# Decay attention with a gated MLP on one Trainium2 core: one decay row of 512 a head, masked in place, and four decay and transposed tiles

## The chip, the cores and the metric

The program runs on one core of one Trainium2 chip, in one launch. The metric is the device time in microseconds (us). The kernel before took 532.27 us, the median of three runs (524.27, 532.27 and 534.39 us).

The engines are named as the profile names them: PE (matrix multiply), PEld (its weight loads), DVE (vector), ACT (scalar and activation), POOL (general purpose), SP (here it only issues DMAs). Each engine runs its own instructions in the order in which they stand in the program, and waits where an operand is not ready.

## The reference

```python
def _attn_ref(q, k, v, f):                       # q, k, v: (8, 8, 576, 64); f: (8, 8, 576)
    scores = 1/sqrt(64) * q @ k^T
    log_f = np.log(np.clip(f, 0.0001, 1.0))
    cum = np.cumsum(log_f, axis=-1)
    decay = cum[:, :, :, None] - cum[:, :, None, :]
    scores = np.where(causal, -1e9, scores + decay)      # causal: key after query
    scores = scores - np.max(scores, axis=-1, keepdims=True)
    attn = np.exp(scores)
    attn = attn / (np.sum(attn, axis=-1, keepdims=True) + 1e-09)
    return attn @ v

def _moe_ref(x, w_val, conv_w, w_out):           # x: (8, 576, 512), heads side by side
    gate_pre = sum over 5 taps of conv_w[k] * x shifted by k
    gate = 1.0 / (1.0 + np.exp(-gate_pre))
    return (gate * (x @ w_val)) @ w_out
```

All arrays are float32. The term `cum[query]` of a row of scores is the same for all keys, so the softmax takes it away again: any number that is constant along a row may be added to the row's decays.

## The kernel before, in words

Two heads of a batch entry make a pair; there are 32 pairs, four to a batch entry. A pair's 576 queries are four blocks of 128, j = 0 to 3, with 128(j + 1) keys each, and a rest of 64 queries with all 576 keys; the rests of both heads share one 128-row tile. The stages of a pair are these.

- Load: `Xr` (queries and keys), `vt` (values), and for pairs 2 to 31 the decays, by a DMA that copies one row of the DRAM table `decd` to 128 partitions: `dm`, 1280 columns a head (the four blocks' 128, 256, 384 and 512 keys behind each other, each block with its own reference), and `dl`, 576 columns for the rest. There are three `dm` tiles.
- Mask: POOL writes -8e9 over the upper triangle of the four diagonal blocks of a `dm` tile, in two `affine_select` instructions of 128x256 (L314), once the tile has landed. The rest's 64 columns get `tri` added (L317, DVE or POOL).
- S: PE multiplies queries by keys into PSUM (`banks`). From pair 4 on the operands are split in a high and a low part (`Xh`, `Xl`; L268 and L397) and three products are made.
- Reduce (L479, DVE): adds the decays to the scores in place and returns each row's extreme; a small instruction then reads that out (`negm`). Exp (L483, ACT) makes `P` and the row sums.
- PT: PE transposes `P` (L511, L529, L530); ACT or DVE copies the result to `pt` (L268), of which there are three.
- PV: PE multiplies `vt` by `pt`; DVE multiplies the result by the inverse row sums (L580), which come as a DMA broadcast through DRAM (`rzd`), into `x`. `xh` and `xl` are its split.
- Convolution: five taps on `x` into `gate` (L616 on DVE for four of them), then a tanh on ACT.
- MoE of a batch entry once its four pairs are through: Mv (`xh`, `xl` by `w_val`), gating on DVE (L648), a split into `hh` and `hl`, Mo (by `w_out`), output copies (L689, L691) and DMAs.

At the start DVE clips `f`, ACT takes the logarithm (L348), ACT loads its second table of functions (L349), DVE makes the running sum (L350), and `ref` (L352) and five scaled copies (L359 on ACT, L361 on DVE) make the table `st`, which two DMAs write to `decd`. Pairs 0 and 1 don't wait for `decd`: PE adds their decays to the scores by a selecting matrix `pick`, and their reduction reads a `dm` tile that holds zeros and the mask. The two weight matrices are decoded on DVE and ACT in eight chunks (L705 to L717) into high and low parts.

What order the instructions stand in on each engine, and which engine does an instruction that several could do, is given by the string `TABLE`: five characters or so for each step, made beforehand by a planner. Every step that `plan_...` adds has a list of what it reads and writes; the table only may order them.

Of the kernel before, what the change touches and what calls it, by code (L numbers as in the profile page):

```python
# [7 lines left out]
F32 = mybir.dt.float32  # L8
# [19 lines left out]
NXR = 3  # L28
R0 = 16
# [5 lines left out]
SW = 1280  # L35
XZ, XK, XW = 512, 640, 1216
# [11 lines left out]
423M15A41s21u14z21t24F24D23R003S11v35I37z44A14G14B24E14H0177t43A21y13x001z24M24C13y23D31A24-
023T034Y054143B13U13P063_44I21H45y449004U034Z11B24O23C31C14J14N13Q24K27v41D24L14P13E25_051E24T24t41G34a21S447016027K17L3482540475g24V15h25525845H31F15
647I13F26117B45e14d15f14W004X17J34b14c35S0135X21K24_11J15V25J046755T250025U15Z25118O45K25L18I48Q45O25P15Q252005R15a44e25M21M25c41L25313G25N11N11O27x45  # L50
Y15k077F382045W17H3832a345-16223H28X16b018Z38411P21Q11R37V0027G38-25l263036c16416f0646r18K46g15E46q26j46h4a147-
26p15i056s19X48W365071U18Y2670321468169015j25m21V29h047_15o16618026a17W27Y27X11X29i2bi47Z16l44f25n36d061W26e19j16n41Y18e008U3980734g2ba49d24h27M014651
Z28116v027R28f1aa1ab39e1ac1ad37S17T27U17N28M47O17P26t008c05992a938d17Q19Z47D48a0686018b28V39a16w21-
22038528716u26I05a7388068915p26x18i0278s18u1bg48v25q26y28j18m48_001649021_18g028t2942bo38k43I16J09119f26F076G09g19_46K2bp2bq3a839629518q4aw058h19719b2
9c19p029q18o46H26L1br1ax2ay1di48w049225r28y00231do45s29318x2an0724i1bc45t1ae06513as28z2ao29l009m1at16N04aq2af29k26z16O0aj28S4al2am1ah26M3ag16Q006R09n0
# [121 lines left out]
def tile_decay_attention_gated_mlp(  # L177
# [643 lines left out]
```

## Time and profile before

| | |
|---|---|
| runs | 524.27, 532.27, 534.39 us |
| profiled execution, its own time | 527.19 us |
| its span, first to last instruction | 525.3 us |
| granted TensorE clock, mean | 0.999 |
| PE, PEld busy | 504.5, 443.6 us |
| DVE, ACT, POOL busy | 438.7, 347.6, 224.3 us |
| DMA traffic | 103.39 MB |

A busy time is the time in which at least one instruction of the engine was under way. Matmuls overlap each other and their ends are modelled. An engine's idle time before an instruction is put down to what ended it.

### The profile page before, as it was taken

Reading aid. Unit: us, or ns where it says so; the run is one execution under the profiler, and the core shown is the slowest. Engines: PE = TensorE matmul, PEld = TensorE weight load, DVE = VectorE, ACT = ScalarE, POOL = GpSimd, SP = SyncE. Lnnn points to the kernel's source line nnn. Section 1 sums busy time; section 2 is a strip of 40 time slices with the busy share of each in tenths; the row PEclk is TensorE's granted clock in tenths of the full one; section 3 lists DMA queues with packets and bytes.
Section 4 is the critical chain, followed back from the end, with each engine's and each line's share of the span. In section 5 each row is a group of like instructions: output and inputs, shape, how many; then the busy total and the mean of one; then the engine's idle time right before and its main releaser. Section 6 shows DMA issues by size and latency. Waiting matters only on the chain. (4 is left out here: it accounts for less than half of the span.)

```text
span 525.3 us, 12611 instructions
## 1 busy us (share of the span) xinstructions
PE 504.5 (96%) x4392; PEld 443.6 (84%) x4392; DVE 438.7 (84%) x1186; ACT 347.6 (66%) x991; POOL 224.3 (43%) x293
## 2 busy tenths in 40 slices
PE   7887999999989999999999998999999999999997
PEld 6555789989988898987899887999898997998885
DVE  6899999898889888898797897898888897868680
ACT  6799998885667665767757776778657664543111
POOL 5248565646352261563326752565454531140110
PEclk9999999999999999999999999999999999999999
DMA  6979898565664676576757386766677544320022
GB/s 212 307 237 325 282 282 288 187 225 157 224 214 136 233 238 190 154 247 198 213 202 271 126 262 219 235 178 225 205 243 259 204 157 144 121 69 2 22 81 100
DMA packets 35022, 103.39 MB, mean 197 GB/s; under 512 B 5072, under 2 KB 5328, under 8 KB 34960
## 3 DMA queue, kind: packets, MB, share of 16 engines
q1 hardware_dynamic: 34960, 102.60, 60.0%
q8 instruction: 34, 0.56, 0.4%
q14 instruction: 28, 0.23, 0.2%
HBM read 92.52 MB, written 10.06 MB: 195 GB/s over the span
## 5 line engine op out<-in xcount | busy, mean ns | idle before, releaser
L483 ACT ACTIVATE P<-banks,negm 128x128 f32<-128x128 f32 (+3 forms) x256 | 133.8, 532 | 38.4 <-DVE negm L479 35.5
L479 DVE CUSTOM_DVE_ANT_0 banks<-banks,dm 128x384 f32<-128x384 f32 (+3 forms) x256 | 120.5, 512 | 10.1 <-PE banks L253 6.6
L268 ACT COPY pt<-banks 128x256 f32<-128x256 f32 (+2 forms) x235 | 94.5, 437 | 41.7 <-PE banks L511 22.7
L253 PE MATMUL banks<-xh,wall 128*128 128x288 f32 x512 | 113.2, 300 | 0.0
L616 DVE SCALAR_TENSOR_TENSOR gate<-x,cw,gate 128x576 f32<-128x576 f32 x128 | 108.9, 857 | 1.1
L253 PE MATMUL banks<-pt,vt 128*64 128x128 f32 (+2 forms) x1408 | 95.8, 290 | 1.9 <-ACT P L483 1.9
L253 PEld LDWEIGHTS banks<-pt,vt 128*64 128x64 f32 x1408 | 84.0, 137 | 13.8 <-ACT P L483 3.1
L511 PE MATMUL banks<-ident,P 128*128 128x128 f32 x640 | 89.0, 277 | 5.5 <-ACT pt L268 2.5
L253 PE MATMUL banks<-wall,hh 128*128 128x512 f32 x288 | 91.9, 400 | 2.0 <-ACT P L483 0.9
L314 POOL TENSOR_SCALAR_AFFINE_SELECT dm<-dm 128x256 f32<-128x256 f32 x122 | 57.6, 498 | 84.0 <-DMA dm<-decd 66.9
L253 PEld LDWEIGHTS banks<-xh,wall 128*128 128x128 f32 x512 | 85.0, 188 | 1.3 <-DVE h L648 0.3
L511 PEld LDWEIGHTS banks<-ident,P 128*128 128x128 f32 x640 | 71.1, 140 | 15.3 <-ACT P L483 4.0
L253 PE MATMUL banks<-xl,wall 128*128 128x288 f32 x256 | 75.4, 295 | 0.0
L397 POOL TENSOR_TENSOR Xl<-Xr,Xh 128x576 fp32r<-128x576 f32 (+1 forms) x41 | 63.0, 1545 | 19.9 <-ACT Xh L268 16.0
L253 PE MATMUL banks<-Xh 128*128 128x288 f32 (+4 forms) x280 | 59.2, 339 | 3.7 <-ACT Pl L483 1.7
L253 PEld LDWEIGHTS banks<-wall,hh 128*128 128x128 f32 x288 | 51.2, 188 | 11.7 <-DVE x L580 1.4
L253 PE MATMUL banks<-wall,hl 128*128 128x512 f32 x144 | 56.4, 391 | 0.0
L253 PE MATMUL banks<-Xh,Xl 128*128 128x288 f32 (+4 forms) x280 | 54.8, 315 | 0.1
L253 PE MATMUL banks<-Xl,Xh 128*128 128x288 f32 (+4 forms) x280 | 54.0, 313 | 0.0
L483 ACT ACTIVATION_READ_ACCUMULATOR P<-banks,negm 128x1 f32 x256 | 52.6, 205 | 0.0
L253 PEld LDWEIGHTS banks<-xl,wall 128*128 128x128 f32 x256 | 48.2, 188 | 0.5
L587 POOL TENSOR_TENSOR xl<-x,xh 128x576 fp32r<-128x576 f32 x20 | 29.2, 1462 | 44.7 <-ACT xh L268 41.0
(95 smaller groups left out, 726.0 us busy)
## 6 DMA issues: line engine op xcount, KB each, us to landing
dm<-decd SPq DMA_DIRECT2D x60, 640.0 KB
Xr<-in_x_dram SPq DMA_DIRECT2D x32, 608.0 KB
vt<-in_v_dram SPq DMA_DIRECT2D x32, 320.0 KB
x<-rzd SPq DMA_DIRECT2D x64, 144.0 KB
out_dram<-ot SPq DMA_DIRECT2D x36, 256.0 KB
dl<-decd SPq DMA_DIRECT2D x60, 144.0 KB
ot<-in_w_val_dram SPq DMA_DIRECT2D x2, 512.0 KB
wu<-in_w_val_dram SPq DMA_DIRECT2D x2, 512.0 KB
```

Of the source, the lines that this page charges most:

```text
L253: nc.tensor.matmul(out, lhsT=lhsT, rhs=rhs, start=start, stop=stop)
L268: (eng.copy if eng is nc.scalar else eng.tensor_copy)(out=out, in_=in_)
L314: nc.gpsimd.affine_select(out=t, in_=t, pattern=[[0, 2], [-1, P]], base=0, channel_multiplier=1, compare_op=ALU.is_ge, fill=-BIG)
L397: eng.tensor_tensor(out=Xl[r][:, a:e], in0=Xr[r][:, a:e], in1=Xh[r][:, a:e].bitcast(F32), op=ALU.subtract)
L479: nc.vector.tensor_tensor_reduce(out=sl, in0=sl, in1=add[:, o:o + ext], op0=ALU.add, op1=ALU.min, scale=-0.125, scalar=3.0e38, accum_out=n ...
L483: nc.scalar.activation(out=dst[:, o:o + ext], in_=bank(key)[:, c0:c0 + ext], func=AF.Exp, bias=negm[r][:, col], scale=-1.0, accum_out=zs[r ...
L511: nc.tensor.transpose(out=bank(key)[:, c:c + P], in_=Pt[m][:, BOFF[b] + P * j:BOFF[b] + P * j + P], identity=ident)
L587: any_("xl", {"POOL": 1.4, "DVE": 0.67}, p, lambda eng: eng.tensor_tensor(out=xl[s], in0=xv, in1=xh[s][:, :].bitcast(F32), op=ALU.subtract ...
L616: eng.scalar_tensor_tensor(out=gt, in0=src, scalar=wt_, in1=gt, op0=ALU.mult, op1=ALU.add)
```

## The change

Each head has one decay row of 576 columns with one reference (the running sum at key 288) in place of five pieces with five references. A pair's head loads only the first 512 columns (128x512, 256 KB, before 640 KB) into one of four `dm` tiles. All four blocks read that tile from its first column. The mask of block j is written over its last 128 columns right before its reduction, by POOL or by DVE (adding `tri4`): block 3 first, then 2, 1 and 0, since block 2 needs the columns that were masked for it, and block 3 needs the same columns unmasked. So each head has the chain mask, reduce, mask, reduce and so on, four of each. The groups of PSUM banks change to fit: blocks 3 and 2, then blocks 1 and 0.

At the start one DVE instruction makes the whole table, and one DMA writes it. The reduction of pairs 0 and 1 reads `mask` and `maskl`. There are four `pt` tiles. The `rzd` DMAs may be issued by ACT as well as by SP. POOL may do convolution taps of the first pairs (the new table gives it none). The whole order is new.

```diff
+REF = S // 2
+NDM = 4
+NPT4 = 4
...
 TABLE = """
-0240040430s010w000c20u040e20f10740g10v030b30F40t010Q40520h20H10i20932g001240k12i00K20n20l10m10z32r0570C33342e30j10o43540I20J20E32h00q40630L10B32n22o12
...
+0d20710930040430q030m010240e20o020520B40D10p010G20M40f10a30E20F20h20630H10I20u30z32Z40J22a002350i22c00j40K20L20O10P20b20R20g10S10X45v40Q20c32h22i12j22
...
-    decd = dram.tile([R, SW + S], F32, name="decd")
-    dm = tiles(NH, [P, SW], F32, "dm")
+    decd = dram.tile([R, S], F32, name="decd")
+    dm = tiles(NDM, [P, L0], F32, "dm")
...
-    pt = tiles(NH, [P, 1600], F32, "pt")
+    pt = tiles(NPT4, [P, 1600], F32, "pt")
...
-            load("dec", 2.3 if i < 6 else 2.05, p + 0.05 * h, dm[m], decd[2 * i + h:2 * i + h + 1, 0:SW].to_broadcast([P, SW]), dk, [("dm", m)])
+            load("dec", 0.85, p + 0.05 * h, dm[(2 * i + h) % NDM], decd[2 * i + h:2 * i + h + 1, 0:L0].to_broadcast([P, L0]), [("decd",)], [("dm", (2 * i + h) % NDM)])
...
-            def sel(m=m):
-                for lo, n, c in ((0, 256, 0), (256, 512, 384)):
-                    t = dm[m][:, lo:lo + 2 * n].rearrange("p (b c) -> p b c", b=2)[:, :, c:c + P]
-                    nc.gpsimd.affine_select(out=t, in_=t, pattern=[[0, 2], [-1, P]], base=0, channel_multiplier=1,
-                                            compare_op=ALU.is_ge, fill=-BIG)
-            pool("sel", 0.8, p + 0.2 + 0.05 * h, sel, [("dm", m)], [("dm", m)])
...
-    dve("st0", 0.12, z, lambda: nc.vector.tensor_scalar(out=ref, in0=cum[:, 0:L0 + 1:P], scalar1=8.0, scalar2=0.0, op0=ALU.mult, op1=ALU.add),
-        kc, [("ref",)])
...
-    for c in cuts:
-        cut(*c)
...
-        load("tabD", (0.35, 0.9)[n], z - 0.5, decd[r0:r1], st[r0:r1], [*ktab, *kst], [("decd", n)])
+    dve("cut0", 0.45, z, lambda: nc.vector.tensor_scalar(out=st, in0=cum, scalar1=cum[:, REF:REF + 1], scalar2=-8.0,
+        op0=ALU.subtract, op1=ALU.mult), kc, kst)
+    load("tabD", 0.5, z - 0.5, decd, st[0:R], kst, [("decd",)])
...
-    SG = (((0, 3, 0), (1, 3, 0), (0, 1, 0), (1, 1, 0)), ((0, 2, 0), (1, 2, 0), (0, 0, 384), (1, 0, 384)), ((None, 0, 224),))
+    SG = (((0, 3, 0), (1, 3, 0), (0, 2, 0), (1, 2, 0)), ((0, 1, 0), (1, 1, 0), (0, 0, 256), (1, 0, 256)), ((None, 0, 224),))
...
+                if u < 2 and not deep:
+                    def sel(eng, t=dm[md][:, ext - P:ext]):
+                        if eng is nc.gpsimd:
+                            eng.affine_select(out=t, in_=t, pattern=[[-1, P]], base=0, channel_multiplier=1, compare_op=ALU.is_ge, fill=-BIG)
+                        else:
+                            eng.tensor_tensor(out=t, in0=t, in1=tri4, op=ALU.add)
+                    any_("sel", {"POOL": 0.3, "DVE": 0.21}, pp - (0.3 if j == 3 else 0.0), sel, [*dkey, ("tri4",)], dkey)
...
-        load("rzw", 0.1, p + 0.03, rzd[i, :, L0:], rt[r][D + 2 * NB:], [("rt", r)], [("rzd", i, 1)])
+        load("rzw", 0.1, p + 0.03, rzd[i, :, L0:], rt[r][D + 2 * NB:], [("rt", r)], [("rzd", i, 1)], early=True)
```

The number and shape of PE's instructions stay as they were (3,630 matmuls as the program issues them). Of the other instructions, counted in the order as built: 60 broadcasts of 128x1280 become 60 of 128x512; 122 masks of 128x256 on POOL become 173 of 128x128 on POOL and 67 of 128x128 on DVE; DVE's output copies (L691) go from 16 to 7 and ACT's from 20 to 29; DVE's 128x512 copies of `pt` with four runs go from 16 to 7 and ACT's from 48 to 57; 25 of the 128 `rzd` DMAs are issued by ACT.

The start, on ACT (`h32` holds the convolution weights and `ot` the first chunk of `w_val`, both still coded; `Pl1` holds `f`). Before:

```order
L348 ACTIVATE Pl1_83<-Pl1_83 128x576
L349 ACT_TABLE_LOAD
L705 ACTIVATE gate1_112<-h32_113 128x20
L359 ACTIVATE gate0_111<-x321_94,ref_127 128x256
L359 ACTIVATE gate0_111<-x321_94,ref_127 128x384
L359 ACTIVATE gate0_111<-x321_94,ref_127 128x128
L359 ACTIVATE gate0_111<-x321_94,ref_127 128x512
L713 ACTIVATE h32_113<-h32_113,ebias_125 128x20
L483 ACTIVATE P0_79,zs0_91<-banks_126,negm0_89 128x256
```

and now:

```order
L714 ACTIVATE gate1_115<-h32_116 128x20
L350 ACTIVATE Pl1_85<-Pl1_85 128x576
L722 ACTIVATE h32_116<-h32_116,ebias_128 128x20
L714 ACTIVATE gate1_115<-ot_125 128x512
L351 ACT_TABLE_LOAD
L722 ACTIVATE ot_125<-ot_125,ebias_128 128x512
L478 ACTIVATE P0_81,zs0_94<-banks_129,negm0_92 128x384
```

Four table copies (L359) are gone; two instructions that need the first chunk of `w_val` (the fourth and sixth row) now stand ahead of the first exp.

The masks of pair 4, on DVE (`dm0` and `dm1` are its two heads now, `dm2` and `dm0` before). Before, the reductions stood in any order, with the masks long done:

```order
L479 ISA banks_126,negm0_89<-banks_126,dm2_70 128x256
L479 ISA negm0_89 128x1
L479 ISA banks_126,negm0_89<-banks_126,dm0_68 128x256
L479 ISA negm0_89 128x1
L479 ISA banks_126,negm0_89<-banks_126,dm2_70 128x512
L479 ISA negm0_89 128x1
L479 ISA banks_126,negm0_89<-banks_126,dm0_68 128x512
```

and now:

```order
L474 ISA banks_129,negm0_92<-banks_129,dm0_69 128x512
L474 ISA negm0_92 128x1
L474 ISA banks_129,negm0_92<-banks_129,dm1_70 128x512
L474 ISA negm0_92 128x1
L485 TENSOR_TENSOR dm0_69<-dm0_69,tri4_66 128x128
L474 ISA banks_129,negm0_92<-banks_129,dm0_69 128x384
L474 ISA negm0_92 128x1
L474 ISA banks_129,negm0_92<-banks_129,dm1_70 128x384
L474 ISA negm0_92 128x1
L625 SCALAR_TENSOR_TENSOR gate0_114<-x321_97,cw_67,gate0_114 128x576
L474 ISA banks_129,negm0_92<-banks_129,dm0_69 128x256
```

The two heads alternate, block 3 first. The mask of block 2 of the first head is one of the 67 on DVE; that of the second head, and the two of block 1, are POOL's. They stand there among POOL's other work (`wall` is a chunk of weights, `xl` and `Xl` are splits):

```order
L590 TENSOR_TENSOR xl1_109<-x321_97,xh1_103 128x576
L751 TENSOR_TENSOR wall_126<-gate1_115,wu_127 128x512
L483 AFFINE_SELECT dm1_70<-dm1_70 128x128
L483 AFFINE_SELECT dm0_69<-dm0_69 128x128
L483 AFFINE_SELECT dm1_70<-dm1_70 128x128
L483 AFFINE_SELECT dm3_72<-dm3_72 128x128
L483 AFFINE_SELECT dm0_69<-dm0_69 128x128
L483 AFFINE_SELECT dm1_70<-dm1_70 128x128
L392 TENSOR_TENSOR Xl0_79<-Xr0_75,Xh0_77 128x576
```

Each of these masks but the fourth row's now has to wait for the reduction of the block before it on DVE, and the next reduction waits for it.

The products of pair 3 (L580, then L583; `x320`), the last that batch entry 0 needs, on DVE. Before:

```order
L479 ISA banks_126,negm1_90<-banks_126,dm1_69 128x384
L479 ISA negm1_90 128x1
L268 COPY pt2_86<-banks_126 128x256
L580 TENSOR_TENSOR x320_93<-banks_126,x320_93 128x192
L717 TENSOR_SCALAR ot_122<-gate1_112 128x512
L490 TENSOR_SCALAR Pl0_82<-zs0_91 128x9
L491 RECIPROCAL Pl0_82<-Pl0_82 128x9
L580 TENSOR_TENSOR x320_93<-banks_126,x320_93 128x384
```

and now:

```order
L474 ISA banks_129,negm0_92<-banks_129,dm1_70 128x128
L474 ISA negm0_92 128x1
L583 TENSOR_TENSOR x320_96<-banks_129,x320_96 128x192
L583 TENSOR_TENSOR x320_96<-banks_129,x320_96 128x384
L492 TENSOR_SCALAR Pl0_84<-zs0_94 128x9
L493 RECIPROCAL Pl0_84<-Pl0_84 128x9
```

Counted from the start, DVE has 182 instructions ahead of the first of these two products before, and 174 now. Of each of the four decoding instructions L707, L709, L711 and L715 one fewer stands ahead of it now, of the reductions one of 128 and one of 384 columns fewer, and `ref` is gone.

## Rows read from the trace of the kernel before

**Rows 1.** The page: span, and each engine's busy time with its share.

```profile
span 525.3 us, 12611 instructions
PE 504.5 (96%) x4392; PEld 443.6 (84%) x4392; DVE 438.7 (84%) x1186; ACT 347.6 (66%) x991; POOL 224.3 (43%) x293
```

**Rows 2.** Stretches: length, busy us of PE, PEld, DVE, ACT, POOL; clock, DMA, GB/s.

```profile
0.00:10.00 10.00, 7.37 (x40) 5.98 (x42) 5.37 (x14) 5.76 (x10) 7.33 (x27) 1.00 0.61 207
10.00:60.00 50.00, 42.97 (x358) 31.16 (x355) 45.60 (x142) 45.63 (x132) 23.85 (x30) 1.00 0.90 286
40.00:80.00 40.00, 35.85 (x359) 29.77 (x357) 37.91 (x112) 39.62 (x112) 26.75 (x31) 1.00 0.92 295
100.00:450.00 350.00, 344.62 (x3096) 307.62 (x3094) 303.95 (x820) 237.06 (x698) 159.99 (x199) 1.00 0.63 206
450.00:500.00 50.00, 49.12 (x409) 44.94 (x408) 36.04 (x79) 17.87 (x42) 7.71 (x6) 1.00 0.16 56
```

**Rows 3.** The timeline of ACT at the start: start us, us, instruction.

```profile
5.82 1.28 ACT L349 ACT_TABLE_LOAD   x1
...
7.08 1.56 PE L253 MATMUL banks<-Xr 64*128 64x512 f32 x8 [1.21 <-DMA Xr<-in_x_dram]
...
9.74 0.47 ACT L483 ACTIVATE P<-banks,negm 128x256 f32<-128x256 f32 x1
...
10.80 0.68 ACT L705 ACTIVATE gate<-ot 128x512 f32<-128x512 uint32 x1
...
13.40 0.75 ACT L713 ACTIVATE ot<-ot,ebias 128x512 int32<-128x512 int32 x1
```

**Rows 4.** DVE by line and shape: xcount, busy us, mean ns, idle before.

```profile
L479 DVE CUSTOM_DVE_ANT_0 banks<-banks,dm 128x384 f32<-128x384 f32 x64 | 36.2, 576 | 3.9 <-PE banks L253 2.4 <-issue 0.4 <-POOL dm L314 0.3
...
L268 DVE COPY pt<-banks 128x512 f32<-128x512 f32 x29 | 19.6, 680 | 1.7 <-PE banks L511 1.4
L479 DVE CUSTOM_DVE_ANT_0 banks<-banks,dm 128x128 f32<-128x128 f32 x64 | 19.4, 312 | 0.8 <-ACT P L483 0.3 <-PE banks L253 0.2
...
L691 DVE TENSOR_SCALAR ot<-banks 128x512 f32<-128x512 f32 x16 | 10.9, 686 | 10.2 <-PE banks L253 5.4 <-DMA out_dram<-ot 4.6
...
L709 DVE SCALAR_TENSOR_TENSOR gate<-gate 128x512 f32<-128x512 int32 x8 | 5.6, 700 | 0.0
L662 DVE TENSOR_TENSOR hl<-h,hh 128x512 fp32r<-128x512 f32 x8 | 5.5, 684 | 0.0
...
L715 DVE SCALAR_TENSOR_TENSOR gate<-ot 128x512 int32<-128x512 int32 x4 | 3.0, 738 | 0.1
...
L317 DVE TENSOR_TENSOR dl<-dl,tri 128x64 f32<-128x64 f32 x10 | 2.5, 253 | 0.0
...
L711 DVE TENSOR_SCALAR ot<-ot 128x512 int32<-128x512 int32 x4 | 1.8, 446 | 0.4 <-ACT gate L705 0.4
L707 DVE TENSOR_SCALAR gate<-ot 128x512 int32<-128x512 int32 x4 | 1.7, 427 | 2.0 <-DMA ot<-in_w_val_dram 1.5 <-DMA ot<-in_w_out_dram 0.4
...
L352 DVE TENSOR_SCALAR ref<-x 128x5 f32<-128x5 f32 x1 | 0.4, 393 | 0.0
```

**Rows 5.** The instructions that write or read `dm`: who waited for them.

```profile
  POOL dm L314: 66.9, 23
...
  DVE banks L479: 1.1, 3
```

**Rows 6.** POOL by line and shape, as rows 4.

```profile
L314 POOL TENSOR_SCALAR_AFFINE_SELECT dm<-dm 128x256 f32<-128x256 f32 x122 | 57.6, 498 | 84.0 <-DMA dm<-decd 66.9 <-DVE x L580 6.8 <-DVE dl L317 5.9
L397 POOL TENSOR_TENSOR Xl<-Xr,Xh 128x576 fp32r<-128x576 f32 x22 | 32.8, 1493 | 14.5 <-ACT Xh L268 10.8 <-DVE Xh L268 3.4
...
L323 POOL TENSOR_SCALAR_AFFINE_SELECT ident<-ident 128x128 f32<-128x128 f32 x1 | 0.3, 292 | 0.1
```

**Rows 7.** Two DVE lines: duration ns least/median/most, first and last start.

```profile
L616 DVE SCALAR_TENSOR_TENSOR gate<-x,cw,gate x128: 756/814/1984, 42.0 to 501.0; 128x576 f32<-128x576 f32 x128
...
L490 DVE TENSOR_SCALAR Pl<-zs x32: 157/170/1512, 22.9 to 477.4; 128x9 f32<-128x9 f32 x32
```

More of the change, by code (lines that the diff above doesn't have):

```diff
@@ L28 @@
 NXR = 3
+NPT = 4
 R0 = 16
@@ L48 @@
[L48 to L55, printed above, removed]
@@ L324, in mk_ident @@
                                 compare_op=ALU.is_equal, fill=0.0)
-    cuts = [(i, BOFF[i], 0, EXT[i]) for i in (3, 1, 2, 0)] + [(NB, SW, 0, S)]
-    ref = const.tile([P, NB + 1], F32, name="ref")
     for h in range(2):
@@ L340, in tile_decay_attention_gated_mlp @@
     for i in range(ND):
[L341 to L344 removed]
+        pool("start", 1.25, z + 0.25, lambda i=i: mk_pick(i), (), kpick[i])
+    any_("start", {"POOL": 0.6, "DVE": 0.42}, z + 0.25, lambda eng: eng.memset(mask, 0.0), (), kmask)
+    pool("start", 0.25, z + 0.27, lambda: nc.gpsimd.affine_select(out=mask[:, L0 - P:], in_=mask[:, L0 - P:], pattern=[[-1, P]], base=0,
+         channel_multiplier=1, compare_op=ALU.is_ge, fill=-BIG), kmask, kmask)
+    any_("start", {"POOL": 0.6, "DVE": 0.42}, z + 0.28, lambda eng: eng.memset(maskl[:, 0:L0], 0.0), (), kmaskl)
     dve("st0", 0.37, z, lambda: nc.vector.tensor_scalar(out=ft, in0=ft, scalar1=1e-4, scalar2=1.0, op0=ALU.max, op1=ALU.min),
@@ L380, in mk_tri, with mk_tri4 @@
                                     compare_op=ALU.is_ge, fill=-BIG)
+    def mk_tri4():
+        nc.gpsimd.memset(tri4, 0.0)
+        nc.gpsimd.affine_select(out=tri4, in_=tri4, pattern=[[-1, P]], base=0, channel_multiplier=1, compare_op=ALU.is_ge, fill=-BIG)
     pool("start", 0.8, z + 0.3, mk_tri, (), [("tri",)])
+    pool("start", 0.65, z + 0.305, mk_tri4, (), [("tri4",)])
+    any_("start", {"POOL": 0.25, "DVE": 0.14}, z + 0.31, lambda eng: eng.tensor_copy(out=maskl[:, L0:], in_=tri), [("tri",), *kmaskl], kmaskl)
     for r in range(NXR):
         pool("start", 0.1, z + 0.4 + r, lambda r=r: nc.gpsimd.memset(x32[r][:, 0:T0], 0.0), (), [("xpad", r)])
-    for r in range(NH):
+    for r in range(NPT4):
         pool("start", 0.1, z + 0.4 + r, lambda r=r: nc.gpsimd.memset(pt[r][D:P, 1536:1600], 0.0), (), [("pt0", r)])
@@ L501, in plan_pt @@
         ms = [(2 * i + h) % NH for h in range(2)]
+        mt = [(2 * i + h) % NPT4 for h in range(2)]
         for n, (h, blocks) in enumerate(((0, (3,)), (1, (3,)), (0, (1,)), (1, (1,)), (0, (2, 0)), (1, (2, 0)))):
@@ L552, in plan_pv @@
         r = i % NQ
-        ms = [(2 * i + h) % NH for h in range(2)]
+        ms = [(2 * i + h) % NPT4 for h in range(2)]
         base = float(i) if i else -5.0
@@ L610, in plan_pv @@
         for n, t in enumerate(reversed(range(KC))):
+            early = i < NPT and n > 0
             def cv(eng, t=t, first=n == 0):
```

213 lines of the change are left out of this document (109 added, 104 removed).

## The prediction

> **What bounds the kernel now.** I read the busy times first, then their shares in stretches of the run, then who waits for the decays, then the rows of the start. The whole-run shares [rows 1] name PE: 504.5 of 525.3 us, so only 20.8 us without a matmul under way. The stretches [rows 2] say where. From 100 to 450 us PE is busy 344.6 of 350 us, DVE 304.0, ACT 237.1, POOL 160.0: here PE sets the pace, and DVE has 46 us idle. From 10 to 60 us it is otherwise: PE 43.0 of 50, DVE 45.6, ACT 45.6, with the DMA engines at 0.90; and from 40 to 80 us ACT is busy 39.6 of 40 and DVE 37.9. No batch entry has all its four pairs yet, so there is little MoE work for PE, while the attention work fills DVE and ACT. So the start is set by DVE and ACT, the long middle by PE. PE's own work does not change, and its clock is at the full level throughout, so a gain must come from the first 80 us or from PE's few gaps later.
>
> **How the time is counted.** The profiled execution took 527.2 us, its span 525.3. The sum is made against 527.2. The runs shown lie from 524.3 to 534.4 with a median of 532.3; the profiled one is nearer their lower end. That spread is 1.9%, so 2% is about what a measurement of this kernel can tell from no change.
>
> **The change part by part.**
>
> Smaller broadcasts. 60 loads lose 384 KB each, 23.6 MB of the run's 103.4. POOL waited 66.9 us for these loads, but POOL is busy 43% and its waiting costs nothing by itself; DVE's reductions waited only 1.1 us, in 3 places, for what touches the tile [rows 5]. The price lies between 0 and -1.1 us; I take -1, since the waits fall where the tiles are reused, and four tiles of which none is reused within two pairs leave more room.
>
> The start. Five table copies and `ref` (0.39 us) become one copy. Against that, the first exp stands behind two ACT instructions on the first chunk of `w_val`, 0.68 and 0.75 us, and behind the second table load, 1.28 us. Before, that exp began at 9.74 us and the chunk was first used at 10.80 us [rows 3]. When the chunk lands the trace doesn't show: not before the operands loaded ahead of it, which PE used from 7.08 us, and not after 10.80. So the first exp begins between 7.08 + 2.71 = 9.8 us and 10.80 + 2.71 = 13.5 us, 0 to 3.8 us later. The 1.43 us of chunk work then no longer stands later on ACT, which is full. Net -1.4 to +2.4 us; I take +1, since a load of 512 KB beside one of 608 KB should land nearer to the later end.
>
> Work ahead of batch entry 0. The first Mv products need pair 3's `x`, and DVE now has 174 instructions ahead of the first product of that pair where it had 182. One weight chunk's decoding moves behind it: 0.427 + 0.700 + 0.446 + 0.738 = 2.3 us. `ref` goes, 0.39 us; two reductions, 0.312 and 0.576 us, stand behind [rows 4]. The other differences (casts and copies fewer, memsets, masks and a wider split more) about cancel by the same kind of rows. That is 3.6 us in a stretch where DVE is busy 95% of the time [rows 2], and between 0 and -3.6 on the path; I take -3, near the full end, because DVE has almost no idle time there that could hide it already.
>
> Masks. POOL does 173 masks of 128x128 where it did 122 of 128x256. One such instruction on another tile took 0.29 us, the wider one 0.50 on average [rows 6]: 50 to 87 us against 61, all on an engine with more than half its time free. DVE gets 67. The nearest rows are the same operation on 64 columns, 0.25 us, and on 512 columns, 0.68 us [rows 4]; 128 columns are near the first, so 0.28 us, 19 us in all, with 17 and 46 as ends. The new order also takes 9 output copies of 0.686 us and 9 copies of `pt` of 0.680 us from DVE, 12.3 us, and some splits. DVE's total is then about +5 us, nearly all in the middle, where it has 46 us idle; ACT's is higher by some 11 us with 113 us idle there [rows 2]. On the path: 0.
>
> Waits of the mask chain. 180 masks now stand behind a reduction of the same head, 58 of them on DVE itself and 122 on POOL. For these 122 the order puts other DVE work between the two reductions in all places but one, as it does for pair 4; a mask of 0.3 us fits beside one reduction of 0.3 to 0.6 us. Ends: 0, and the price of the second rival below. I take +1 us, in the first 80 us, where DVE has no room.
>
> Buffers and queues. A fourth `pt` tile and `rzd` DMAs on ACT's queue can only shorten waits. PE had 0.9 us idle from 450 to 500 us, where the last pair comes through DRAM [rows 2]. 0 to -0.9 us; I take -1 with the waits on `pt` that I can't see apart.
>
> Sum: -1 + 1 - 3 + 0 + 1 - 1 = -3. 527.2 - 3 = 524 us.
>
> **Rivals.** *The start opens up.* If DVE and ACT were held there by late loads more than by their own work (DMA at 0.90 to 0.92 speaks for it, ACT's 39.6 of 40 us busy against it), smaller loads would let the first 80 us run as the middle does. PE lacks 7.0 us from 10 to 60 us by its matmuls. By weight loads it lacks more: PEld is busy 31.2 of 50 us there, 0.62, and 307.6 of 350, 0.88, in the middle [rows 2]; 50 x (1 - 0.62/0.88) = 14.8 us. With the better part of that, 13 us: 514 us, and 512 to 520 by these bounds. The Trainium skill, "Perfetto Trace Analysis", section on identifying the most-contended engine, says that matmul busy time is a bad measure of headroom and that the share of weight loads is the better one. By matmuls 20.8 us are free in the whole run, by weight loads 81.7 us [rows 1]. The trace agrees as far as the two rows differ most just where PE has little to do; by the rule this rival would be dearer than by PE's idle time alone.
>
> *The mask chain stalls DVE.* POOL runs in order and is busy 26.8 of 40 us from 40 to 80 us, 0.67, with pieces of 1.5 us [rows 2, 6]. A mask that comes up at a random moment would wait 0.67 x 0.75 = 0.5 us behind such a piece, and DVE after it. By the order some 27 of the 122 masks belong to the first 80 us: 27 x 0.5 = 13.6 us, against 2.1 us that DVE has idle from 40 to 80 us, so +11.5. In the middle 95 x 0.46 x 0.75 = 33 us would fall into 46 us of idle time; if a quarter of it comes through to PE, +8. 527.2 - 4 + 11.5 + 8 is 543, and 538 with half of each. It decides once DVE waits more than 2 us for POOL before 80 us. Against it: the order places long pieces of POOL elsewhere, as for pair 4, and other DVE work between. For it: DVE and POOL do hold each other up at times. A convolution tap of 0.81 us took up to 1.98, and an instruction on nine columns, 0.17 us, up to 1.51 [rows 7]. The Trainium skill, "SBUF — State Buffer", says that DVE and POOL share a port pair, and that a DVE instruction with two SBUF inputs and a POOL instruction that reads SBUF exclude each other for a whole instruction. By that rule a convolution tap placed as cover would itself hold up the mask that it should cover; 25 of the 122 have such an instruction right behind the reduction, 25 x 0.81 = 20 us, of which the cover behind it takes most. The traces' extremes agree with it; how often it strikes here no row shows.
>
> *The change does nothing to the time*: fewer bytes, hidden anyway, and another order of equal worth. 527 us.
>
> **How the numbers follow.** Forecast 524 us (517 to 532), 0.47. No effect, 527, 0.08. Start opens up, 514 (508 to 520), 0.29. Chain stalls, 541 (535 to 547), 0.16. The range reaches from 510, which leaves out a third of the third case's span, about 0.08, to 538, which leaves out two thirds of the last, about 0.11. Against 527.2 us, faster by over 2% is below 516.7: most of the third case and a little of its neighbours' tails, 0.28. Slower by over 2% is above 537.7: most of the last case and a tail, 0.15. Within: 0.57.
>
> **What would show it.** In the profile after: DMA traffic near 80 MB and POOL's wait for `dm` far below 66.9 us. The first exp between 9.8 and 13.5 us. The first Mv product some 2 us earlier than before, with ACT still full from 40 to 80 us; if PE's busy share from 10 to 60 us rises above 0.92, the first rival holds. DVE's idle time before the reductions put down to POOL below 3 us in all; above 10 us, the second holds. DVE busy near 444 us, ACT near 360. I am wrong if the middle, 100 to 450 us, changes its pace by more than 1%: none of my terms lies there.

## The result

The changed kernel took 522.38 us (median of 519.61, 520.75, 524.00 and 524.46) where the kernel before took 531.38 on the same chip: ratio 0.9879, 95% interval 0.9839 to 0.9918. The ratio compares fast runs alone, so it is not that of the two medians, 0.983. That is faster by 1.2%, and within 2%. The forecast was 524.

The profiled execution took 524.0 us. Its page, to be read against [rows 1], shows span and busy times:

```profile
span 522.3 us, 12784 instructions
PE 504.3 (97%) x4392; PEld 444.1 (85%) x4392; DVE 444.2 (85%) x1215; ACT 363.3 (70%) x1021; POOL 229.1 (44%) x349
...
DMA packets 35009, 79.49 MB, mean 152 GB/s; under 512 B 5056, under 2 KB 5312, under 8 KB 34944
```

The engines' totals are near where the prediction put them: DVE 444 (444 forecast), ACT 363 (360), and 79.5 MB of traffic (80). The stretches of the changed kernel, with the columns of [rows 2]:

```profile
0.00:10.00 10.00, 6.36 (x28) 4.54 (x30) 4.13 (x13) 2.66 (x5) 3.08 (x17) 1.00 0.62 209
10.00:60.00 50.00, 43.15 (x338) 31.96 (x334) 42.07 (x128) 42.70 (x119) 21.86 (x40) 0.93 0.69 213
40.00:80.00 40.00, 36.09 (x353) 29.40 (x353) 37.16 (x105) 37.48 (x107) 28.44 (x40) 1.00 0.67 209
100.00:450.00 350.00, 347.94 (x3162) 312.42 (x3161) 315.48 (x868) 260.00 (x746) 167.89 (x247) 1.00 0.52 160
450.00:500.00 50.00, 50.00 (x418) 46.24 (x417) 37.98 (x85) 18.24 (x44) 9.27 (x8) 1.00 0.12 42
```

The reader is to see two things. From 10 to 60 us the granted clock is 0.93 where it was 1.00 before. And PE, which had 5.4 us without a matmul between 100 and 450 us, now has 2.1.

Stretches at fixed times don't tell where the gain lies, as one kernel may be further on in its work. So I sorted each trace's matmuls by start, counted each with the median time from its start to the next one's for its shape (about 460 us in all), and read off when that sum passed a mark. Differences to the kernel before at equal PE work, in us, for the profiled executions of all kernels that the argument rests on (minus is ahead):

```
PE work done         20    60   100   140   180   220   260   300   380   440   end
kernel before, at  31.0  82.0 125.0 168.0 212.0 258.0 300.0 345.0 432.0 497.0 522.0
changed            +5.0  +4.6  +5.9  +5.0  +5.1  +1.8  +3.7  +1.2  -0.5  -2.3  -3.0
no_stall           +1.7  +1.7  +3.6  +2.9  +2.8  -0.5  -0.2  -2.7  -4.4  -5.8  -6.5
no_masks           +1.3  +0.4  +2.2  +0.9  +0.7  -1.6  -1.5  -4.0  -5.1  -7.0  -7.7
late_loads_back    +1.2  +3.1  +6.0  +4.9  +7.7  +4.7 +11.6 +13.6 +15.6 +13.8 +13.1
less_load          -0.2  +1.2  +1.4  +1.3  +1.2  -0.6  -0.6  -2.5  -2.5  -3.2  -3.2
act_fwd            +1.6  +2.6  +3.2  +2.3  +6.4  +9.6 +10.0  +9.9 +11.8 +11.3 +10.7
dve_back           +3.3  +2.8  +4.1  +6.8 +10.9  +8.9 +13.2 +11.1  +9.7 +10.5  +9.8
```

Each row is one execution; the four runs of the changed kernel alone lie 5 us apart, so a difference between two rows is worth no more than the runs' ratios bear out.

The changed kernel is 5 us behind when a mere 20 us of PE's work is done, stays there until 180, and then gains 8 us. Both halves differ from the prediction, which had about 3 us won before batch entry 0 and nothing later; only the sum agrees.

### The profile page after: what moved, and what is told of

Its sections match the earlier page's. It is cut to its first block, busy times and chain, and to the rows that moved or that the text cites. A ratio compares the mean times of both kernels' runs of the same rounds, so it can differ in the third digit from the quotient of the medians.

```text
span 522.3 us, 12784 instructions
## 1 busy us (share of the span) xinstructions
PE 504.3 (97%) x4392; PEld 444.1 (85%) x4392; DVE 444.2 (85%) x1215; ACT 363.3 (70%) x1021; POOL 229.1 (44%) x349
## 4 chain that ended last, share of the span: by engine, by line
PE 76%; DMA 3%; DVE 3%; ACT 1%; issue 1%; SPq 0%; ACTq 0%; POOL 0%; DVEq 0%
PE banks L262 63%; PE banks L514 11%; PE banks L532 2%; DMA Xr<-in_x_dram 2%; DMA x<-rzd 1%; DVE gate L625 1%; PE banks L533 1%; DVE banks L474 1%; ACT P L478 0%; ACT pt L277 0%; DVE dm L485 0%; DMA rzd<-rt 0%; DVE Pl L492 0%; DVE pt L277 0%; SPq L289 0%
## 5 line engine op out<-in xcount | busy, mean ns | idle before, releaser
L478 ACT ACTIVATE P<-banks,negm 128x256 f32<-128x256 f32 (+3 forms) x256 | 134.4, 532 | 41.0 <-DVE negm L474 36.0
L474 DVE CUSTOM_DVE_ANT_0 banks<-banks,dm 128x512 f32<-128x512 f32 (+3 forms) x240 | 115.3, 504 | 11.4 <-PE banks L262 4.2
L483 POOL TENSOR_SCALAR_AFFINE_SELECT dm<-dm 128x128 f32<-128x128 f32 x173 | 64.9, 385 | 133.6 <-DVE negm L474 105.5
L277 ACT COPY pt<-banks 128x512 f32<-128x512 f32 (+2 forms) x242 | 98.5, 448 | 31.1 <-PE banks L514 18.8
L625 DVE SCALAR_TENSOR_TENSOR gate<-x,cw,gate 128x576 f32<-128x576 f32 x128 | 111.3, 876 | 1.1
L514 PEld LDWEIGHTS banks<-ident,P 128*128 128x128 f32 x640 | 72.4, 142 | 15.8 <-ACT pt L277 4.2
L392 POOL TENSOR_TENSOR Xl<-Xr,Xh 128x576 fp32r<-128x576 f32 (+1 forms) x36 | 58.6, 1631 | 18.9 <-ACT Xh L277 8.5
L262 PE MATMUL banks<-Xh 128*128 128x288 f32 (+4 forms) x280 | 56.6, 335 | 1.0 <-ACT P L478 0.6
L671 POOL TENSOR_TENSOR hl<-h,hh 128x64 fp32r<-128x64 f32 (+2 forms) x32 | 33.4, 1055 | 53.6 <-ACT hh L277 27.9
L262 PE MATMUL banks<-Xh,Xl 128*128 128x288 f32 (+4 forms) x280 | 53.2, 315 | 0.0
```

The lines of the kernel that those rows point to most:

```text
L262: nc.tensor.matmul(out, lhsT=lhsT, rhs=rhs, start=start, stop=stop)
L277: (eng.copy if eng is nc.scalar else eng.tensor_copy)(out=out, in_=in_)
L392: eng.tensor_tensor(out=Xl[r][:, a:e], in0=Xr[r][:, a:e], in1=Xh[r][:, a:e].bitcast(F32), op=ALU.subtract)
L474: nc.vector.tensor_tensor_reduce(out=sl, in0=sl, in1=add, op0=ALU.add, op1=ALU.min, scale=-0.125, scalar=3.0e38, accum_out=negm[r][:, col])
L478: nc.scalar.activation(out=dst[:, o:o + ext], in_=bank(key)[:, c0:c0 + ext], func=AF.Exp, bias=negm[r][:, col], scale=-1.0, accum_out=zs[r ...
L483: eng.affine_select(out=t, in_=t, pattern=[[-1, P]], base=0, channel_multiplier=1, compare_op=ALU.is_ge, fill=-BIG)
```

## Experiments

Two theories were tested for the start (the order of its steps loses time) and two for the later gain (fewer bytes let other transfers land earlier; the new order and its balance of engines). All ratios are to the kernel before on the same chip.

**The start.** The changed kernel's DVE, timeline from 24 us:

```profile
25.93 0.43 DVE L716 TENSOR_SCALAR gate<-ot 128x512 int32<-128x512 int32 x1 [1.70 <-DMA ot<-in_w_val_dram]
26.27 0.54 DVE L277 COPY pt<-banks 128x256 f32<-128x256 f32 x2
```

ACT behind it:

```profile
26.84 0.26 ACT L277 COPY rt<-banks 9x128 f32<-9x128 f32 x1 [3.50 <-DVE pt L277]
```

and PE behind ACT:

```profile
28.98 2.29 PE L262 MATMUL banks<-Xr 128*128 128x288 f32 x4 [3.50 <-ACT pt L277]
```

DVE stands at the decoding of the second chunk of `w_val`, whose transfer is late, while the copies of `pt` behind it are ready; ACT waits for these copies, and PE for ACT's. Then the clock falls. The wait at the chunk by itself is not new: in the kernel before DVE also waited 1.54 us for it, until 25.78 us, but PE's longest wait behind that was 0.91 us, and its clock stayed at 1.00. What differs is what stands behind the decoding. The stretch of half clock:

```profile
27.88:34.70 6.82, 5.72 (x21) 4.85 (x21) 4.54 (x13) 4.67 (x13) 0.00 (x0) 0.50 0.71 241
```

Three kernels move steps of the table: the numbers in brackets are put right behind the last number. The moves, on the changed kernel:

```diff
+MOVES = [((73, 72, 75, 76), 217)]                              # no_stall: second chunk's decode behind the pt copies
+MOVES = [((16,), 15), ((50, 51, 53, 54, 52), 148)]             # table_early: table load behind Ln, first chunk's decode behind the second exp
+MOVES = [((16,), 15), ((50, 51, 53, 54, 52), 148), ((73, 72, 75, 76), 217)]   # both_moves
```

> The changed kernel with the second of the two moves alone: the decode of the second weight chunk behind the copies of the first transposed decays. Theory: TensorE's 3.5 to 4 us without work at 24 to 29 us shrink to under 1.5 us, the granted clock stays full after it, and 2 to 4 us less than the changed kernel, ratio 0.980 to 0.984. Rival (the idle time is owed to the late start of everything, the decode only fills it): the idle time stays within 1 us and the ratio is that of the change, 0.984 to 0.992.

Measured: 519.92 us, ratio 0.9801 [0.978, 0.9821], below the change's interval. It is 3.3 us ahead of the changed kernel at the first mark and keeps it to the end. PE's longest wait between 23 and 31 us is 1.3 us, and the clock stays at 1.00:

```profile
30.85 0.33 PE L549 MATMUL banks<-ident,Pl 128*73 128x128 f32 x1 [1.30 <-ACT pt L293]
```

The mean granted clock was 1.000 in all four of its runs, and 0.993, 0.996, 1.000 and 0.997 in those of the changed kernel. The theory holds; by its median it is the fastest of all versions run, ahead of both kernels.

> The changed kernel with the first of the two moves alone: the table load directly behind Ln on ACT, the first weight chunk's decode behind the second exponential. Theory: the first exponential 2 to 2.8 us earlier (about 10 us of the span) and TensorE ahead by as much until 24 us; the stall at 24 to 29 us stays, as the late chunk still stands ahead of the copies, and takes most of it back: 0 to 2 us less than the changed kernel, ratio 0.984 to 0.989. Rival (the start is all set by the first exponential): 2.5 us less or more, ratio below 0.984, and the stall gone with it.

Measured: 523.18 us, ratio 0.9873 [0.9852, 0.9894].

> The changed kernel with two steps of its start moved: the table load now stands directly behind Ln on ACT and the first weight chunk's decode behind the second exponential; the decode of the second weight chunk now stands behind the copies of the first transposed decays on DVE. Theory (the changed kernel has lost about 5 us by 36 us of its span, half of it because the first exponential comes 2.8 us later, half because DVE waits 1.7 us for a late chunk ahead of the copies that TensorE needs, and the granted clock halves for 6.8 us behind that): the first exponential at about 10 us of the span, no stretch at half the clock between 25 and 35 us, and 3 to 5 us less than the changed kernel, 517 to 519 us where the kernel before takes 531, ratio 0.974 to 0.978. Rival (what is lost at the start is given back later anyway, since a later wait of the weights or of the first batch entry absorbs it): the ratio stays that of the change, 0.984 to 0.992.

Measured: 523.40 us, ratio 0.9871 [0.985, 0.9891]. The ratio of table_early lies in the range that I gave it, that of both_moves does not, and the mechanism fell in both. The first exp came only 0.5 us (both_moves, 12.0 us) and 0.9 us (table_early, 11.7 us) earlier than the 12.5 us of the changed kernel, where I had expected 2 to 2.8: with the table load out of the way ACT waited 2.8 us for the reduction. And the decode, put later, stood in the way there: PE then waited 2.3 us for ACT at 17 us, where it waited 0.4 us without that move. Timeline of PE in both_moves:

```profile
17.62 0.44 PE L530 MATMUL banks<-ident,P 128*128 128x128 f32 x2 [2.30 <-ACT P L494]
```

The next kernel keeps the good move, puts the first x load on SP's queue behind `f`, as before, and the table load behind Ln:

```diff
+MOVES = [((7,), 2), ((16,), 15), ((73, 72, 75, 76), 217)]
+OTHER = {7: 'SP'}
```

> The changed kernel with three moves at its start: the second weight chunk's decode behind the copies of the first transposed decays (as in the run with 0.9801), the first x load on SP's queue behind the loads of f as in the kernel before, and the table load directly behind Ln. Theory (f lands 1.7 us later in the changed kernel because the x load on ACT's queue shares the DMA engines with it): f's clip at 4.4 to 5 us of the span instead of 6.2, the first exponential 1.5 to 2.5 us earlier, about 10.5 us, and 1 to 2 us less than the run without the two last moves: 517.5 to 519 us at 530 before, ratio 0.976 to 0.979. Rival (the first exponential stands behind the weight decode on DVE anyway): ratio 0.978 to 0.982, as without them.

Measured: 520.05 us, ratio 0.9824 [0.9783, 0.9866]; no better than no_stall. The clip of `f` moved from 6.43 us (no_stall) to 5.35, but the convolution weights then landed later, their first decode stands ahead of Ln on ACT, and the row of ACT shows it:

```profile
7.35 0.22 ACT L734 ACTIVATE gate<-h 128x20 f32<-128x20 uint32 x1 [5.26 <-DMA h<-in_conv_w_dram]
7.48 0.67 ACT L370 ACTIVATE Pl<-Pl 128x576 f32<-128x576 f32 x1
```

So Ln began at 7.48 us, later than the changed kernel's 6.65, and the first exp came at 13.46 us. The theory falls; the ratio lies just above the rival's range.

**The loads, taken from the kernel before.**

```diff
+    def LD(i):
+        return SW if i < 4 else L0
...
-            load(..., dm[m], decd[2 * i + h:2 * i + h + 1, 0:SW].to_broadcast([P, SW]), ...)
+            load(..., dm[m][:, 0:LD(i)], decd[2 * i + h:2 * i + h + 1, 0:LD(i)].to_broadcast([P, LD(i)]), ...)
```

> The kernel before, but from the fourth pair on it loads 512 of the 1280 decay columns a head (the other columns of the tile keep older decays, so this part of the computation is left out): 56 x 384 KB less traffic, the order of the work as before. Theory 1 (the middle of the changed kernel runs about 9 us faster than before because the broadcast loads are shorter and other loads land earlier): 5 to 9 us less than the kernel before, ratio 0.983 to 0.990. Theory 2 (the middle is faster through the new order and the work taken from DVE to ACT, the loads were hidden): within 2 us, ratio 0.996 to 1.004.

Measured: 525.97 us, ratio 0.9915 [0.9882, 0.9947]: 4.5 us less, between the theories. In its profile, too, it gains 4.5 us between the marks of 140 us and the end (+1.3 to -3.2). The loads were not hidden in the old order: 4.5 us hang on 56 of them, 22.0 MB. How much of the new order's 8 us that is, this run can't say. One place shows how. The kernel before, 312 to 322 us (length, busy us of PE, PEld, DVE, ACT, POOL; clock, DMA, GB/s), then its timeline there, a row of DVE and one of PE:

```profile
312.00:322.00 10.00, 8.39 (x56) 7.00 (x56) 6.52 (x14) 4.92 (x15) 2.57 (x4) 1.00 0.84 272
```

```profile
319.10 0.69 DVE L691 TENSOR_SCALAR ot<-banks 128x512 f32<-128x512 f32 x1 [3.13 <-DMA out_dram<-ot]
...
320.20 0.50 PE L253 MATMUL banks<-Xh 64*128 64x512 f32 x1 [1.34 <-DVE h L648]
```

The same stretch and the same DVE row of less_load:

```profile
312.00:322.00 10.00, 9.71 (x73) 8.44 (x71) 8.21 (x25) 6.97 (x20) 2.48 (x4) 1.00 0.59 202
```

```profile
316.65 0.69 DVE L694 TENSOR_SCALAR ot<-banks 128x512 f32<-128x512 f32 x1 [1.31 <-DMA out_dram<-ot]
```

and of the changed kernel:

```profile
312.00:322.00 10.00, 10.00 (x74) 9.27 (x72) 9.51 (x26) 6.35 (x20) 4.37 (x8) 1.00 0.80 256
```

DVE stood at an output copy until an earlier output had been stored; with fewer bytes the store landed sooner, and PE's stall was gone. DVE's waits for two kinds of transfer show the same over the whole run, in the kernel before

```profile
DVE x L580 <- DMA x<-rzd: 8.3, 7, 4.4
DVE ot L691 <- DMA out_dram<-ot: 4.6, 2, 3.1
```

and in less_load (us, times, longest):

```profile
DVE x L583 <- DMA x<-rzd: 4.9, 2, 4.5
DVE ot L694 <- DMA out_dram<-ot: 1.9, 2, 1.3
```

What each of these waits is worth at the end of the kernel was not tested.

**The loads, put back into the change.** A transfer of 384 KB, from `x` to scratch in DRAM, ahead of each head's broadcast, for all pairs that have one (loads_back), then from pair 4 on (late_loads_back):

```diff
+                    if i >= 4:                  # this line in late_loads_back alone
+                        nc.sync.dma_start(out=extra, in_=src)
+                    nc.sync.dma_start(out=out, in_=row)
...
+            plan.dma(..., dec(dm[d], decd[...].to_broadcast([P, L0]), junk[h], x[i][:, 0:SW - L0]), ...)
```

> The changed kernel with the traffic that it saved put back: ahead of each head's broadcast load a transfer of 384 KB on the same queue, from x to a scratch tile that nothing reads (60 of them, 23.6 MB). Measured so far: the kernel before with that traffic taken away from the fourth pair on is 4.4 us faster. Theory 1 (traffic is half of what the middle of the changed kernel gained): 2.5 to 5 us more than the changed kernel, ratio to the kernel before 0.993 to 0.998, the loss between 150 and 450 us. Theory 2 (the new order does not need it, four decay tiles cover late loads): within 1.5 us of the changed kernel, ratio 0.985 to 0.991.

Measured: 546.65 us, ratio 1.0337 [1.0291, 1.0383]; both theories far too low. Half of the loss lies in the first 125 us, where the second weight chunk is later still: PE waits 8.55 us, does 0.57 and 0.89 us of work in two stretches of 5 us (25 to 35 us), and is granted 0.50 of its clock behind that.

> The changed kernel with the extra 384 KB ahead of a head's broadcast from the fourth pair on alone, the mirror image of the run that took them from the kernel before (-4.4 us). By the earlier run with all 60 of them (+24 us, of it 12.6 us by the first 100 us of TensorE's work): the first 100 us unchanged within 1 us, and 8 to 12 us more than the changed kernel, ratio 1.003 to 1.011. Rival (the order catches up once the start is on time; what traffic is worth is the same in both orders): 3 to 6 us more, ratio 0.993 to 0.999.

Measured: 540.28 us, ratio 1.0191 [1.0143, 1.0239], 17 us more than the changed kernel, above theory and rival. By the number of bytes that is four times the price that they have in the kernel before, but these are not the same transfers: the extra ones also write to DRAM, as the pages of the kernel before (first) and of this run show.

```profile
HBM read 92.52 MB, written 10.06 MB: 195 GB/s over the span
```

```profile
HBM read 90.95 MB, written 31.75 MB: 228 GB/s over the span
```

So the 17 us are no price of the broadcasts themselves. DVE's reductions by shape, in the changed kernel (first) and here:

```profile
L474 DVE CUSTOM_DVE_ANT_0 banks<-banks,dm 128x384 f32<-128x384 f32 x60 | 33.3, 574 | 2.4 <-POOL dm L483 0.8 <-PE banks L262 0.2
L474 DVE CUSTOM_DVE_ANT_0 banks<-banks,dm 128x256 f32<-128x256 f32 x60 | 25.6, 435 | 2.4 <-PE banks L262 1.4 <-POOL dm L483 0.2
```

```profile
L483 DVE CUSTOM_DVE_ANT_0 banks<-banks,dm 128x384 f32<-128x384 f32 x60 | 33.2, 573 | 6.1 <-POOL dm L492 4.2 <-DVE dm L494 0.5 <-PE banks L263 0.2
L483 DVE CUSTOM_DVE_ANT_0 banks<-banks,dm 128x256 f32<-128x256 f32 x60 | 25.6, 435 | 5.2 <-POOL dm L492 3.9 <-PE banks L263 0.5
```

and the masks on POOL here:

```profile
L492 POOL TENSOR_SCALAR_AFFINE_SELECT dm<-dm 128x128 f32<-128x128 f32 x173 | 65.0, 386 | 145.0 <-DVE negm L483 92.7 <-DMA dm<-decd 46.7 <-DMA vt<-in_v_dram 2.8
```

POOL waits 46.7 us for `dm` (24.4 in the changed kernel), and DVE waits 10.0 us in 15 places for POOL's masks (2.2 us in 7):

```profile
DVE banks L483 <- POOL dm L492: 10.0, 15, 2.3
```

The chain of load, mask and reduction, which the second rival feared, does stall DVE once the loads are late. Part of the price is the extra transfers' own: SP waited 10.0 us for them in all (they share two scratch tiles), and everything behind stood in its queue. And in two later stretches of 3.4 us each (from 305.05 and 342.59 us) PE was granted 0.50, which makes up to 3.4 of the 17 us.

**The masks left out.**

```diff
-                    def sel(eng, t=dm[md][:, ext - P:ext]):
-                        ...
+                    def sel(eng):
+                        pass
```

> The changed kernel with the 240 masks of the decay tiles left out (173 on POOL, 67 on DVE; positions ahead of the diagonal are not cut off then, so this part of the computation is left out). The prediction's terms: the masks cost 0 as work and about 1 us as waits, so 0 to 2 us less than the changed kernel, ratio to the kernel before 0.984 to 0.990. Rival 1 (the mask chain stalls DVE, 14 us in the prediction): 8 us less or more, ratio below 0.975. Rival 2 (after the run in which 10 us of work given back to DVE cost 14 us: the 67 masks on DVE, some 20 us of its time, are paid for by TensorE): 8 to 20 us less too, and then DVE's busy time is down by about 20 us and TensorE's waits on DVE with it, while in rival 1 the 2.2 us that DVE waits for masked tiles are what goes.

Measured: 521.47 us, ratio 0.9838 [0.9797, 0.9879], as the prediction's terms had it: both rivals fall. In the profile it is 4.7 us ahead of the changed kernel, but 3.7 of these are won by the first mark, where not one mask has been left out on DVE yet (the first stands at 41.8 us in the changed kernel): in this execution, as in that of late_loads_back, the weight chunk landed in time, PE's wait was 1.65 us instead of 3.50, and the clock stayed full. So by these two executions the masks cost about 1 us, and the rest is the late chunk; by the ratios it is 2 us, with intervals that overlap. DVE's busy time fell by 21 us, to 423.2, and this bought almost nothing:

```profile
PE 502.3 (97%) x4392; PEld 443.0 (86%) x4392; DVE 423.2 (82%) x1148; ACT 362.3 (70%) x1021; POOL 167.9 (32%) x176
```

**Engines.** The output copies and the casts of `h` to `hh` in the changed kernel go back to the engines of before, 25 of them to DVE and 7 to ACT (and the other way round in the kernel before for act_fwd):

```diff
+            e = OTHER.get(n, e)      # OTHER: the engines of 32 steps
```

> The changed kernel in its order, but the output copies and the casts of h to hh on the engines that did them before: 25 of them from ACT to DVE, 7 from DVE to ACT. By the rows of DVE (687 and 450 ns) some 10 us of work go back to DVE. Theory (the other half of the middle's gain is work taken from DVE, which is what TensorE waits for most in the kernel before): 2 to 5 us more than the changed kernel, ratio to the kernel before 0.992 to 0.998, TensorE's waits on DVE up. Rival (the share of the two engines is not what counts): within 1.5 us, ratio 0.985 to 0.991.

Measured: 536.38 us, ratio 1.0125 [1.0077, 1.0173], 14 us more than the change and far above theory and rival. DVE's busy time rose by 8.7 us.

> The kernel before in its order and with its loads, but the output copies and the casts of h to hh on the engines that do them in the changed kernel: 25 from DVE to ACT, 7 from ACT to DVE, some 10 us of work off DVE. Theory (less work on DVE is worth time in either order, as giving it back cost 14 us): 2 to 6 us less than the kernel before, ratio 0.988 to 0.996. Rival (an order is made for its engines, any swap inside it costs): 3 to 14 us more, ratio 1.005 to 1.026; then the 14 us say little of the balance by itself.

Measured: 534.77 us, ratio 1.0097 [1.0061, 1.0132]: 5 us slower, though DVE's busy time fell from 438.7 to 433.2. The rival holds: these 32 steps cost when they change engines inside an order, in both directions. The theory of the balance by itself falls, also since DVE's total is higher in the changed kernel than before.

> The kernel before with both: 512 of the 1280 decay columns a head loaded from the fourth pair on (the other columns keep older decays, that part is left out), and the output copies and casts of h to hh on the engines of the changed kernel. Theory (the middle's 9 us are loads plus balance): 6 to 10 us less than the kernel before, ratio 0.981 to 0.989, about the sum of the two single runs. Rival (swaps inside an order cost): the single run's loss, less 4 us.

Measured: 533.83 us, ratio 1.0082 [1.0046, 1.0118]: the loss of act_fwd, with no gain from the loads that its interval shows. The two don't add.

**Three decay tiles.**

```diff
-NDM = 4
+NDM = 3
```

A step whose inputs are not ready in the table's order is put back until they are.

> The changed kernel with three decay tiles instead of four; a step whose inputs are not there yet in the order is put back until they are, else the order stands. Theory (the fourth tile lets a head's decays be loaded and masked a head earlier, POOL is slow and has much to do): 1 to 4 us more than the changed kernel, with DVE's idle time before the row minimum of banks and dm up from 2.2 us. Rival (three were enough before with one mask fewer, and they are now): within 1.5 us, ratio 0.985 to 0.991.

Measured: 600.49 us, ratio 1.1333 [1.1271, 1.1394]. Much more than expected, and not a clean price of the fourth tile: the steps that were put back also moved others. It says that this order rests on four tiles, no more.

## Why the prediction was right in sum and wrong in its parts

**Start, +1 by the first exp: right in size, one step short.** The first exp came at 12.51 us, inside 9.8 to 13.5, behind the chunk as predicted. By the executions in which the second chunk landed in time, 1.2 to 1.3 us are lost there at equal PE work. But a second path stood close behind, and no term has it: in the changed order the clip of `f` began at 6.15 us (4.42 before), and with the chunk work out of the way (table_early) the first exp came only 0.9 us earlier. That the size fits is in part luck. What I did not follow at all was the second chunk: I priced a chunk's decode by DVE's work alone (2.3 us) and never asked what waits behind one whose transfer is late. Where it was late, another 3.7 us went, by PE's wait and by the half clock after it.

**Work ahead of batch entry 0, -3: this step failed.** The first Mv did come 2.9 us earlier (66.3 us; 69.2 before), as predicted, but at that moment PE as a whole was 5 us behind. I took one milestone as the path; the new order had only done that piece of work earlier and other work later (the first `h` of the MoE began at 87.6 us, 74.2 before). ACT was not full any more from 40 to 80 us either (37.5 of 40).

**Shorter broadcasts, -1, ends 0 and -1.1: this step failed.** less_load puts it at -4.5 us in the old order. My bound counted only who waits for `dm`. What gained, as far as DVE's waits show it, were waits for other transfers: the row of L691 in [rows 4] names 4.6 us of waiting for `out_dram<-ot` (1.9 in less_load), and I read that row only for the duration of a copy; those for `x<-rzd` went from 8.3 to 4.9 us.

**Masks, 0, and their waits, +1: right.** By no_masks about 1 us together in the profiles, and by the ratios 2 us that the intervals don't part from 0. The who-waited view of the changed kernel, to be read against [rows 5]:

```profile
  POOL dm L483: 24.4, 5
...
  DVE banks L474: 2.2, 7
```

2.2 us is below the 3 that I named, so the second rival is refuted here; late_loads_back, at 10.0 us, shows that its mechanism was real. The price of one mask on DVE was off, see below.

**The middle, 0: wrong.** I said that I would be wrong if it changed its pace by more than 1%. Between the marks of 100 and 440 us of PE's work the kernel before needs 372 us and the changed one 8.2 less, 2.2%. I had seen no more to gain there than PE's few gaps, 5.4 us, and even that was the wrong measure: between these marks PE's idle time fell from 5.9 to 1.8 us, half of the gain, and the other half was time that the profile counts as busy (the same 350 us held 3096 matmuls before and 3162 now, in [rows 2] and above). What earned it stays open. The loads were worth 4.5 us in the old order; in the new one no run prices them. Engine swaps and extra loads both break the order, so they don't say which of its moves counts, and the fourth `pt` tile and the `rzd` DMAs on ACT's queue were not tested by themselves. (The term for buffers and queues, -1, was bounded by 0.9 us of PE's idle time from 450 to 500 us, and that is gone: 50.00 of 50. No run tells whose merit it is.) PE's waits in the middle are shorter all over. The first rows of PE's waits between 100 and 450 us, before and then changed:

```profile
PE banks L253 <- ACT Pl L483: 1.7, 2, 1.4
PE banks L253 <- DVE h L648: 1.6, 2, 1.3
PE banks L253 <- ACT P L483: 0.9, 1, 0.9
```

```profile
PE banks L514 <- DVE pt L277: 0.7, 1, 0.7
PE banks L262 <- ACT P L478: 0.6, 1, 0.6
```

**The first rival** (the start opens up) asked for PE's share above 0.92 from 10 to 60 us; it is 0.86, and 0.88 in no_stall, where the clock stays full. Fewer bytes did not open the start. The share of weight loads, 31.96 of 50 us, has hardly moved either.

So in the profiled executions, 524.0 us against 527.2, the sum was right because two misjudged parts cancelled: a start that lost up to 5 us where I had a gain, and a middle that gained 8 where I had nothing. That it met so well is luck once more: the one is among the slower runs of its kernel and the other among the faster, and by the ratio the change is worth some 6 us (4.3 to 8.5 by its interval), not 3.

## What to carry to other kernels

Before a transfer is called hidden, list every wait on any transfer in the trace, not only those on the tile that changes: with fewer bytes in one load, waits for others fell here. When a step that needs a DMA stands ahead of ready work on an in-order engine, price the wait with all that stands behind it, TensorE's clock included; moving four steps was worth 0.8% here. And one milestone that comes earlier proves nothing: compare two orders at equal work of the engine that bounds them.

## What the runs showed of the hardware

PE's clock fell behind short pauses. With 3.50 us of waiting before 28.98 us the changed kernel was granted 0.50, the 1.2 GHz level, from 27.88 to 34.70 us. With 1.67 us (late_loads_back), 1.65 us (no_masks) or at most 1.30 us (no_stall) at the same place it stayed at 1.00; with 2.34 us (dve_back) it was 0.70 from 30 to 35 us. The rows of late_loads_back, no_masks and dve_back:

```profile
27.57 1.24 PE L263 MATMUL banks<-Xr 128*128 128x288 f32 x4 [1.67 <-ACT pt L278]
```

```profile
27.64 1.24 PE L262 MATMUL banks<-Xr 128*128 128x288 f32 x4 [1.65 <-ACT pt L277]
```

```profile
27.98 1.24 PE L266 MATMUL banks<-Xr 128*128 128x288 f32 x4 [2.34 <-ACT pt L281]
```

At 17 us it went either way: 2.3 us of waiting left the clock full in both_moves and not in table_early. The stretch from 15 to 20 us of the one and then of the other:

```profile
15.00:20.00 5.00, 2.70 (x24) 2.06 (x23) 4.87 (x18) 4.15 (x15) 1.70 (x4) 1.00 0.97 298
```

```profile
15.00:20.00 5.00, 2.71 (x15) 2.27 (x17) 4.94 (x18) 4.41 (x16) 2.03 (x5) 0.77 0.96 273
```

The length of one wait does not decide it alone. In early_f PE waited 0.90 us before 49.57 and 0.78 us before 51.45 us, no longer wait stood near, and the clock fell all the same; in no_stall the same two waits of 0.90 and 0.78 us left it full. The stretch in early_f:

```profile
51.60:55.00 3.40, 3.40 (x20) 2.57 (x21) 3.40 (x11) 3.40 (x12) 3.01 (x6) 0.50 0.86 262
```

What else decides, these runs don't show. At the start the landing of one chunk goes with some 3.7 us, and the profiled executions with one and the same order of steps there (changed, no_masks, late_loads_back) differ by as much.

A mask on DVE took 292 ns by the median but 404 on average, 27.0 us for 67 where I had 19:

```profile
L485 DVE TENSOR_TENSOR dm<-dm,tri 128x128 f32<-128x128 f32 x67 | 27.0, 404 | 1.0
```

All 23 masks of over 320 ns ran beside a POOL instruction (so did 15 of the 44 shorter ones), and the seven longest ended 144 to 151 ns after a split or a cast on POOL had ended. The longest of them in DVE's timeline, and the split in POOL's:

```profile
424.56 1.45 DVE L485 TENSOR_TENSOR dm<-dm,tri 128x128 f32<-128x128 f32 x1
```

```profile
423.71 2.15 POOL L392 TENSOR_TENSOR Xl<-Xr,Xh 128x640 fp32r<-128x640 f32 x1
```

The split ends at 425.86 us, the mask at 426.01. The Trainium skill, "SBUF — State Buffer", section "SBUF: two separate sides", says that such a pair excludes each other for a whole instruction; this trace agrees, with 0.15 us from the one's end to the other's. The mask itself loses up to 1.15 us by it, and by no_masks little of it reaches the end of the kernel.
